# A head's 48 rows as 32 and 16: other transposes and other transfers for the attention tensors

## The chip, the cores and the metric

The kernel runs on one core of a Trainium2 chip. The metric is the device time in microseconds. Three runs of the kernel before took 797.55, 798.67 and 798.87 us (median 798.67). The profile comes from a further execution, which took 796.42 us; its span from the first to the last instruction is 794.7 us.

## The reference: what is computed

Three stages follow one another, all in fp32.

```
q, k, v, alpha: [4, 8, 768, 48]
state = alpha[t][:, None] * state + k[t][:, None] * v[t]   # 48 x 48 per head, t = 0..767
y[t]  = q[t] @ state
x = y as [3072, 384]
h = x @ w_in (384 x 2048);  g = (a0 + a1 h + a2 h^2 + a3 h^3) / (1 + |b0||h| + |b1| h^2 + 1e-6);  x = g @ w_out
h = x @ w_in2 (384 x 1024); s = h * softmax(h); x = layernorm(s) * g_ln @ w_out2
```

## The kernel before: tiles, stages and what sets the order

The sequence is cut into six chunks of 128 tokens, and each chunk into two halves of two batches; the twelve halves are numbered 0 to 11. A half has four slots of four heads, so its alpha, k and q arrive as tiles `ra`, `rk` and `rq` of 128 partitions (four slots of 32, each with four tokens in a row) by 16 x 48 values. Within a half the recurrence becomes matmuls: the running product P of alpha and its reverse scan R scale q and k (on partitions: the 48 rows of a head; along them: tokens), TensorE forms the scores `sc`, multiplies them with v into `y`, and makes the update `u` of the state `Sbd`.

For halves 0 and 1 TensorE does the transposes. For halves 2 to 11 the function `a_dve` does them on VectorE, block by block of 32 x 32 (`transpose_in`, the transposes of lines 290 and 295): they write columns four values apart, since a raw row holds four tokens. Then come the scans (lines 308 and 317), the product of k and R (line 320) and the transposes of that product back to tokens as rows (line 324), which read four values apart and write consecutively. The product of q and P is on GpSimd (line 335). Both results go through DRAM to change partitions. `kb_d` (line 329) carries the keys back into `kns` (`a_move`, line 282). `qk_d` (line 337) carries q and k into `qks` (`a_move_qk`, line 276), where the two heads of a pair lie on partitions 0 to 47 and 64 to 111 for the scores. `qk` before has three blocks per pair of heads: 32 rows of the one, 16 and 16 rows of both, 32 rows of the other.

The first network (`m_up`, `m_down`) runs 96 units of 512 tokens by 128 hidden columns: nine matmuls into `hp` (line 590), a chain on ScalarE and VectorE (lines 595 to 621), a split into `gh` on ScalarE and `gl` on GpSimd (lines 623, 624), and nine matmuls into `x2p` (line 636). Beside the early units `w1_group` loads the fp64 weights into staging tiles `st`, of which there are two by then (line 531), VectorE converts them to fp32 (lines 535 to 539), and ScalarE and GpSimd split them (lines 545, 546). The second network (lines 700 to 786) follows at the end, with transposes of its own (line 750).

The instructions of each engine run in the order in which a scheduler put them before the launch. It works from its own estimate of times, so an edit in one place can move others. SyncE (SP) issues nearly all transfers, in order: one that has to wait holds up all behind it. The pools say which tiles share memory: `ra` and `rq` are one buffer in turn, and so are the two `st`.

Of the kernel before, what the change touches and what calls it, by code (L numbers as in the profile page):

```python
# [7 lines left out]
F32 = mybir.dt.float32  # L8
# [5 lines left out]
ALU = mybir.AluOpType  # L14
# [16 lines left out]
def kernel(  # L31
# [15 lines left out]
    nc = tc.nc  # L47
# [5 lines left out]
    CH = 128  # L53
# [99 lines left out]
    def network(fast):  # L153
# [7 lines left out]
        if fast:  # L161
            att = tc.tile_pool(name="att", bufs=1, side="right")
            ap_ = att.__enter__()
            ps_a = tc.tile_pool(name="ps_a", bufs=2, space=PSUM, side="right")
            ps_ap = ps_a.__enter__()
            ident = ap_.tile([128, 128], F32, name="ident")
            nc.gpsimd.memset(ident, 0.0)
            nc.gpsimd.affine_select(
                out=ident, in_=ident, pattern=[[-1, 128]], compare_op=ALU.not_equal, fill=1.0, base=0, channel_multiplier=1
            )  # L170
            zero = ap_.tile([128, CH], BF16, name="zero")
            nc.vector.memset(zero, 0.0)
            NB6 = 6
            PER = CH + 1
            QW = 4 * CH + 2
# [28 lines left out]
        class Half:  # L204
            def __init__(self, i):
                if i == 1:
                    t = [borrow(3, 1024 * p, [B, 2 * CH]) for p in range(2)]
                    self.q = [t[p][:, :, :CH] for p in range(2)]
                    self.k = [t[p][:, :, CH:] for p in range(2)]
                    end = ap_.tile([128, B, 2], F32, name="end1")  # L210
                    self.end = [end[:, :, p] for p in range(2)]
                    self.ends = _view(end[:], 0, [[2, B], [1, 2], [0, D]])
                    self.kn = borrow(2, 0, [B * 192 + 16])
                else:
                    self.q = [qks[:, :, CH * p:CH * p + CH] for p in range(2)]
                    self.k = [qks[:, :, 256 + CH * p:256 + CH * p + CH] for p in range(2)]
                    self.end = [qks[:, :, 512 + p] for p in range(2)]
                    self.ends = _view(qks[:], 512, [[QW, B], [1, 2], [0, D]])
# [53 lines left out]

        def a_move_qk(i):
            qk, kb = moved[i]
            for m, i0, n, d0 in ((0, 0, 32, 0), (1, 0, 16, 32), (1, 16, 16, 64), (2, 0, 32, 80)):
                nc.sync.dma_start(out=qks[d0:d0 + n], in_=qk[m].rearrange("b i x -> i b x")[i0:i0 + n])
            yield

        def a_move(i):
            kb = moved.pop(i)[1]  # L280
            v_load(i)
            nc.sync.dma_start(
                out=kns[:, :B * 192].rearrange("p (b x) -> p b x", b=B), in_=kb[:].rearrange("b t x -> t b x")
            )
            yield

        def transpose_in(raw, dst, off, pstep, mstep):
            r0 = raw[:]
            for m, o in ((0, 0), (2, 192 + 16)):
                nc.vector.transpose(  # L290
                    out=_view(dst, off + m * mstep, [[pstep, 2], [1, 4], [4, 32]]),
                    in_=_view(r0, o, [[384, 2], [48, 4], [1, 32]]),
                )
            for p in range(2):
                nc.vector.transpose(
                    out=_view(dst, off + mstep + p * pstep, [[1, 4], [4, 32]]),
                    in_=_view(r0, p * 384 + 32, [[48, 4], [160, 2], [1, 16]]),
                )

        def a_dve(i):  # L300
            ra = raws.pop((i, "ra"))
            nc.vector.memset(_view(alT[:], PER, [[PER, NB6], [1, 2]]), 0.0)
            watch(i, ra)
            transpose_in(ra, alT[:], 1, 3 * PER, PER)
# [5 lines left out]
            qk = ap_.tile([128, 3, QW], F32, name="qk", tag="qk")  # L310
            qv = [_view(qk[:], x * 256, [[CH, 2], [QW, 3], [1, CH]]) for x in range(2)]
            end = _view(qk[:], 512, [[1, 2], [QW, 3]])
            nc.vector.tensor_scalar(end, _view(P[:], CH, [[3 * PER, 2], [PER, 3]]), P_MIN, None, ALU.max)
            nc.vector.reciprocal(_view(d2[:], CH - 1, [[3 * PER, 2], [PER, 3]]), end)
# [4 lines left out]
            transpose_in(raws.pop((i, "rk")), qk[:], 256, CH, QW)  # L319
            nc.vector.tensor_tensor(qv[1], qv[1], _view(R, 0, [[3 * PER, 2], [PER, 3], [1, CH]]), ALU.mult)  # L320
            yield
            kb = R[:, :768].rearrange("p (r x) -> p r x", r=4)
            for p in range(2):
                nc.vector.transpose(  # L324
                    out=_view(kb, 96 * p, [[32, 3], [192, 4], [1, 32]]),
                    in_=_view(qk[:], 256 + CH * p, [[QW, 3], [1, 4], [4, 32]]),
                )
            kb_d = dram.tile([B, CH, 192], F32, name="kb_d", tag="kb_d", bufs=2)
            nc.sync.dma_start(
                out=kb_d[:].rearrange("b (j r) x -> (b j) (r x)", r=4), in_=R[:, :768]  # L330
            )
            yield
            Pv = _view(P[:], 1, [[3 * PER, 2], [PER, 3], [1, CH]])
            transpose_in(raws.pop((i, "rq")), qk[:], 0, CH, QW)
            marks[i, 2] = nc.gpsimd.tensor_tensor(qv[0], qv[0], Pv, ALU.mult)
            qk_d = dram.tile([3, B, 32, QW], F32, name="qk_d", tag="qk_d", bufs=2)
            nc.sync.dma_start(out=qk_d[:].rearrange("m b i x -> (b i) m x"), in_=qk)
            moved[i] = (qk_d, kb_d)
            yield
        vts = {}  # L340
# [715 lines left out]
```

## Time and profile before

| | |
|---|---|
| median of three runs | 798.67 us (797.55 to 798.87) |
| profiled execution | 796.42 us, span 794.7 us |
| PE (TensorE matmul) busy | 732.0 us, 92% of the span |
| DVE (VectorE) busy | 643.2 us, 81% |
| ACT (ScalarE) busy | 535.5 us, 67% |
| POOL (GpSimd) busy | 359.5 us, 45% |
| chain that ended last | PE 45%, DVE 27%, ACT, DMA and "issue" 7% each |

The shares are means over stages of different kind. Halves 2 to 11 have their VectorE part between 44 and 460 us; from 500 us on the attention is over. A row of a timeline gives the start, the duration, the engine, the line, the operation and what it writes and reads; a duration runs to the end of an instruction, and the next one may start before that, so what an instruction takes of its engine is the distance from its start to the next one's start. In brackets stands how long the engine had been idle and what ended the wait.

### The profile page before, as it was taken

What the parts mean: (1) busy time and instruction counts of PE and PEld (TensorE: products, weight loads), DVE (VectorE), ACT (ScalarE), POOL (GpSimd) and SP (SyncE); (2) the same over time, 40 slices, a digit from 0 to 9 for tenths busy, and PEclk for the clock granted to TensorE, in tenths of its full rate; (3) what the DMA queues carried; (4) which work ended last, traced back from release to release, by engine and by line L of the source; (5) the groups of instructions that cost most, each with busy time, mean ns of one, the idle gap of its engine ahead of it and who ended that gap; (6) DMA issues with size and microseconds to landing.
All of it is one profiled execution on the core that took longest, in us unless ns stands there. A gap on an engine that the chain in (4) does not pass through costs nothing.

```text
span 794.7 us, 13903 instructions
## 1 busy us (share of the span) xinstructions
PE 732.0 (92%) x4976; PEld 606.9 (76%) x4976; DVE 643.2 (81%) x1110; ACT 535.5 (67%) x983; POOL 359.5 (45%) x306
## 2 busy tenths in 40 slices
PE   4864986999999989999999999999999999999996
PEld 3753765787777877687777788888888989998996
DVE  5999999979799998979897976567877698777630
ACT  2335756787787868788878879788775555455541
POOL 3256776856555344545454334243242524352322
PEclk9767898999999999999999999999999999999998
DMA  7956466365837275445826160460014443542552
GB/s 172 268 165 187 126 185 134 98 129 164 208 94 179 94 210 143 134 106 162 197 81 160 64 122 15 144 255 0 1 42 106 138 107 100 145 97 60 137 122 69
DMA packets 87279, 101.75 MB, mean 128 GB/s; under 512 B 34464, under 2 KB 63136, under 8 KB 87200
## 3 DMA queue, kind: packets, MB, share of 16 engines
q1 hardware_dynamic: 87104, 100.67, 48.0%
q8 instruction: 41, 0.67, 0.4%
q14 instruction: 38, 0.31, 0.1%
q10 hardware_dynamic: 96, 0.10, 0.0%
HBM read 60.59 MB, written 27.56 MB: 111 GB/s over the span
## 4 chain that ended last, share of the span: by engine, by line
PE 45%; DVE 27%; ACT 7%; DMA 7%; issue 7%; POOL 3%; SPq 3%; DVEq 0%; POOLq 0%; ACTq 0%
PE h L710 13%; PE op L774 12%; PE x2p L636 10%; PE hp L590 9%; DVE ft L539 2%; POOL gl L624 2%; SPq L266 2%; DVE p L616 2%; DVE w L619 2%; DVE alT L324 2%; DVE ft L538 2%; DVE qk L290 2%; DVE p L621 2%; DVE hp L620 2%; DVE ft L535 1%
## 5 line engine op out<-in xcount | busy, mean ns | idle before, releaser
L590 PE MATMUL hp<-xt,g 128*128 128x512 f32 x864 | 226.2, 404 | 16.7 <-DVE p L621 7.7
L590 PEld LDWEIGHTS hp<-xt,g 128*128 128x128 f32 x864 | 163.7, 193 | 59.5 <-DVE p L621 14.2
L624 POOL TENSOR_TENSOR gl<-p,gh 128x512 fp32r<-128x512 f32 x96 | 129.1, 1344 | 175.1 <-ACT gh L623 101.4
L636 PE MATMUL x2p<-gh,g 128*128 128x512 f32 x576 | 196.0, 395 | 0.6 <-ACT gh L623 0.6
L636 PEld LDWEIGHTS x2p<-gh,g 128*128 128x128 f32 x576 | 108.3, 189 | 26.3 <-ACT gh L623 1.4
L636 PE MATMUL x2p<-gl,g 128*128 128x512 f32 x288 | 113.6, 394 | 1.4 <-POOL gl L624 1.4
L774 PE MATMUL op<-w2oh,room 128*128 128x384 f32 x384 | 101.8, 339 | 0.1
L766 POOL TENSOR_TENSOR room<-room,room 128x1024 fp32r<-128x1024 f32 x22 | 53.6, 2438 | 102.2 <-ACT room L765 98.2
L619 DVE SCALAR_TENSOR_TENSOR w<-w,co,hp 128x512 f32<-128x512 f32 x84 | 61.8, 736 | 42.8 <-ACT hp L618 42.4
L710 PE MATMUL h<-w2ih,x 128*128 128x512 f32 x288 | 90.8, 394 | 0.0
L597 ACT ACTIVATE p<-hp,co 128x512 f32<-128x512 f32 x96 | 65.9, 687 | 13.9 <-POOL gl L624 13.4
L618 ACT ACTIVATE hp<-ah 128x512 f32<-128x512 f32 x84 | 50.1, 597 | 32.9 <-DVE p L616 32.2
L616 DVE SCALAR_TENSOR_TENSOR p<-p,co,hp 128x512 f32<-128x512 f32 x84 | 61.7, 734 | 12.7 <-ACT p L597 12.2
L598 ACT ACTIVATE w<-ah,co 128x512 f32<-128x512 f32 x96 | 69.3, 723 | 3.1 <-DVE hp L620 2.9
L774 PEld LDWEIGHTS op<-w2oh,room 128*128 128x128 f32 x384 | 70.0, 188 | 1.7 <-DVE room L766 0.5
L595 ACT ACTIVATE ah<-hp 128x512 f32<-128x512 f32 x96 | 56.7, 590 | 15.9 <-PE hp L590 15.8
L636 PEld LDWEIGHTS x2p<-gl,g 128*128 128x128 f32 x288 | 54.3, 189 | 14.5 <-POOL gl L624 2.6
L623 ACT ACTIVATE gh<-p 128x512 fp32r<-128x512 f32 x96 | 59.9, 624 | 8.1 <-PE x2p L636 3.0
L774 PE MATMUL op<-w2ol,room 128*128 128x384 f32 x192 | 65.0, 339 | 0.0
L621 DVE SCALAR_TENSOR_TENSOR p<-p,co,hp 128x512 f32<-128x512 f32 x84 | 62.2, 740 | 1.2
L710 PEld LDWEIGHTS h<-w2ih,x 128*128 128x128 f32 x288 | 53.9, 188 | 11.7
L617 ACT ACTIVATE ah<-w,co 128x512 f32<-128x512 f32 x84 | 60.6, 722 | 1.3
(168 smaller groups left out, 1281.1 us busy)
## 6 DMA issues: line engine op xcount, KB each, us to landing
room<-room SPq DMA_DIRECT2D x96, 128.0 KB, 2.3
qk_d<-qk SPq DMA_DIRECT2D x10, 771.0 KB, 4.0
st<-in_moe_w_in_dram SPq DMA_DIRECT2D x15, 512.0 KB, 4.9
st<-in_moe_w_out_dram SPq DMA_DIRECT2D x18, 384.0 KB, 4.2
qks<-qk_d SPq DMA_DIRECT2D x20, 257.0 KB, 5.1
x<-x_d SPq DMA_DIRECT2D x18, 256.0 KB, 3.7
out_dram<-o SPq DMA_DIRECT2D x94, 48.0 KB, 1.6
ra<-in_alpha_dram SPq DMA_DIRECT2D x44, 96.0 KB, 2.5
```

The source lines that it names most:

```text
L590: last["PE", u] = nc.tensor.matmul(hp, lhsT=w[:, kt, 128 * o:128 * o + 128], rhs=xts[c][:, kt, xx, :], start=(kt == 0 and w is hi and xx = ...
L597: nc.scalar.activation(p, hp, AF.Square, bias=co[:, 7:8])
L598: nc.scalar.activation(w, ah, AF.Square, bias=co[:, 6:7])
L616: nc.vector.scalar_tensor_tensor(p, p, a1, hp, ALU.add, ALU.mult)
L617: nc.scalar.activation(ah, w, AF.Ln, bias=rest)
L619: nc.vector.scalar_tensor_tensor(w, w, rest, hp, ALU.add, ALU.mult)
L621: fin[u] = nc.vector.scalar_tensor_tensor(p, p, a0, hp, ALU.add, ALU.mult)
L623: last["ACT", u] = nc.scalar.activation(gh, p, AF.Copy)
L624: last["POOL", u] = nc.gpsimd.tensor_tensor(gl, p, gh[:].bitcast(F32), ALU.subtract)
L636: nc.tensor.matmul(x2ps[c][d], lhsT=w[:, o, 128 * d:128 * d + 128], rhs=gg, start=(f == 0 and w is hi and gg is gh), stop=(f == NF1 - 1 an ...
L710: nc.tensor.matmul(hp[:, 512 * n:512 * n + 512], lhsT=x2s[c][:, kt, x, CH * b:CH * b + CH], rhs=w2[w][:, kt, 512 * n:512 * n + 512], start ...
L774: nc.tensor.matmul(op, lhsT=x[:, 128 * f:128 * f + 128], rhs=w2[w][:, f, :], start=(f == 0 and x is hi and w == "oh"), stop=(f == NF2 - 1 ...
```

## The change: 32 and 16 rows

Every head's 48 rows are now 32 and 16. `qk` has six blocks of 257 columns: four with 32 rows of one head each, two with 16 rows of two heads. The numbers of instructions and transfers for one of the halves 2 to 11:

| step | before | now |
|---|---|---|
| transposes of `ra`, `rk` and `rq`, each | 256, 256, 128, 128 elements | 512, 256 elements |
| transposes of the keys back | 384, 384, read four apart | 512, 128, 128, read consecutively |
| write to `qk_d` | 1 transfer | 3 transfers |
| reads from `qk_d` to `qks` | 2 of 32 rows, 2 of 16 rows | 2 of 32 rows, 4 of 16 rows |
| read from `kb_d` to `kns` | 1 transfer of 128 partitions | 4 transfers of 32 partitions |

```diff
         def a_move_qk(i):
             qk, kb = moved[i]
-            for m, i0, n, d0 in ((0, 0, 32, 0), (1, 0, 16, 32), (1, 16, 16, 64), (2, 0, 32, 80)):
-                nc.sync.dma_start(out=qks[d0:d0 + n], in_=qk[m].rearrange("b i x -> i b x")[i0:i0 + n])
+            for j in range(2):
+                nc.sync.dma_start(out=qks[64 * j:64 * j + 32], in_=qk[j].rearrange("b i x -> i b x"))
+            for j in range(2):
+                for p in range(2):
+                    nc.sync.dma_start(
+                        out=qks[64 * j + 32:64 * j + D, :, QB * p:QB * p + QB],
+                        in_=qk[2].rearrange("b i x -> i b x")[16 * p:16 * p + 16, :, QB * j:QB * j + QB],
+                    )
             yield
...
-            nc.sync.dma_start(
-                out=kns[:, :B * 192].rearrange("p (b x) -> p b x", b=B), in_=kb[:].rearrange("b t x -> t b x")
-            )
+            for g in range(4):
+                nc.sync.dma_start(
+                    out=kns[32 * g:32 * g + 32, :B * 192].rearrange("j (b x) -> j b x", b=B),
+                    in_=kb[:, :, 192 * g:192 * g + 192].rearrange("b j x -> j b x"),
+                )
+            yield
+
+        def transpose_in(raw, dst, off, step):
+            r0 = raw[:]
+            nc.vector.transpose(
+                out=_view(dst, off, [[step, 4], [1, 4], [4, 32]]), in_=_view(r0, 0, [[48, 16], [1, 32]])
             )
...
+            nc.vector.transpose(
+                out=_view(dst, off + 4 * step, [[step, 2], [1, 4], [4, 32]]),
+                in_=_view(r0, 32, [[48, 8], [384, 2], [1, 16]]),
+            )
...
             kb = R[:, :768].rearrange("p (r x) -> p r x", r=4)
-            for p in range(2):
+            nc.vector.transpose(
+                out=_view(kb, 0, [[48, 4], [192, 4], [1, 32]]), in_=_view(qk[:], CH, [[QB, 4], [1, CH]])
+            )
+            for j in range(2):
                 nc.vector.transpose(
-                    out=_view(kb, 96 * p, [[32, 3], [192, 4], [1, 32]]),
-                    in_=_view(qk[:], 256 + CH * p, [[QW, 3], [1, 4], [4, 32]]),
+                    out=_view(kb, 48 * j + 32, [[192, 4], [96, 2], [1, 16]]),
+                    in_=_view(qk[:], QB * (4 + j) + CH, [[1, CH]]),
                 )
...
             qk_d = dram.tile([3, B, 32, QW], F32, name="qk_d", tag="qk_d", bufs=2)
-            nc.sync.dma_start(out=qk_d[:].rearrange("m b i x -> (b i) m x"), in_=qk)
+            for j in range(2):
+                nc.sync.dma_start(
+                    out=qk_d[j].rearrange("b i (p x) -> (b i) p x", p=2), in_=_view(qk[:], QB * j, [[QW, 2], [1, QB]])
+                )
+            nc.sync.dma_start(out=qk_d[2].rearrange("b i x -> (b i) x"), in_=_view(qk[:], 2 * QW, [[1, QW]]))
             moved[i] = (qk_d, kb_d)
```

The edit also moves instructions, since the scheduler orders everything again. SP's queue at half 2 read like this before (`kb_d` and `qk_d` are the writes of half 2, `kns` and `qks` its reads, `ra`, `rk` and `rq` loads for half 3, `st` the loads of weight tiles):

```order
L531 DMA st<-in_moe_w_in_dram 128x512 x2
L329 DMA kb_d<-alT 128x768
L266 DMA ra<-in_alpha_dram 32x4x192 x3
L282 DMA kns<-kb_d 128x4x192
L337 DMA qk_d<-qk 128x3x514
L266 DMA ra<-in_alpha_dram 32x4x192
L531 DMA st<-in_moe_w_in_dram 128x512
L276 DMA qks<-qk_d 32x4x514
L276 DMA qks<-qk_d 16x4x514 x2
L276 DMA qks<-qk_d 32x4x514
```

The same place of SP's queue in the changed kernel:

```order
L542 DMA st<-in_moe_w_in_dram 128x512
L338 DMA kb_d<-alT 128x768
L290 DMA kns<-kb_d 32x4x192 x4
L267 DMA ra<-in_alpha_dram 32x4x192
L345 DMA qk_d<-qk 256x1x257 x2
L348 DMA qk_d<-qk 128x514
L267 DMA ra<-in_alpha_dram 32x4x192
L277 DMA qks<-qk_d 32x4x514
L267 DMA ra<-in_alpha_dram 32x4x192
L277 DMA qks<-qk_d 32x4x514
L280 DMA qks<-qk_d 16x4x257 x4
L542 DMA st<-in_moe_w_in_dram 128x512 x2
```

Of the three loads of weight tiles (`st`) that stood around this place, two came ahead of `kb_d` and one ahead of `qks`; now one comes ahead of `kb_d`, and the two others behind the last read of `qks` (one more load of `ra` stands between).

VectorE's order at half 2 before, from the transposes of the keys back on (`rq` is the last raw tile of half 2, lines 535, 538 and 539 convert weight tiles, lines 608 to 621 belong to the units):

```order
L324 STREAM_TRANSPOSE alT<-qk 128x3x4x32 x2
L295 STREAM_TRANSPOSE qk<-rq 128x4x32 x2
L539 SCALAR_TENSOR_TENSOR ft<-lent_175,fp 128x384
L290 STREAM_TRANSPOSE qk<-rq 128x2x4x32
L535 TENSOR_SCALAR ft<-st 128x512
L538 SCALAR_TENSOR_TENSOR ft<-st,ft 128x512
L539 SCALAR_TENSOR_TENSOR ft<-st,ft 128x512
L608 SCALAR_TENSOR_TENSOR hp<-p,co,hp 128x512
L535 TENSOR_SCALAR ft<-st 128x512
L616 SCALAR_TENSOR_TENSOR p<-p,co,hp 128x512
```

The same place of VectorE's order in the changed kernel, from the last transpose of `rq`:

```order
L301 STREAM_TRANSPOSE qk<-rq 128x2x4x32
L549 SCALAR_TENSOR_TENSOR fp<-lent_175,fp 128x384
L550 SCALAR_TENSOR_TENSOR ft<-st,fp 128x384
L550 SCALAR_TENSOR_TENSOR ft<-lent_175,fp 128x384
L546 TENSOR_SCALAR ft<-st 128x512
L549 SCALAR_TENSOR_TENSOR ft<-st,ft 128x512
L550 SCALAR_TENSOR_TENSOR ft<-st,ft 128x512
L619 SCALAR_TENSOR_TENSOR hp<-p,co,hp 128x512
L627 SCALAR_TENSOR_TENSOR p<-p,co,hp 128x512
L507 TENSOR_TENSOR Sbd<-u,end 48x8x48 x2
L624 SCALAR_TENSOR_TENSOR hp<-hp,co,ah 128x512
L630 SCALAR_TENSOR_TENSOR w<-w,co,hp 128x512
```

Three instructions on weight tiles that stood ahead of the last transpose of `rq` now stand behind it. The second tile `st` (`ft<-st 128x512`), which was converted between lines 608 and 616 of the first units, is now converted behind line 630, which was line 619.

## Rows read from the trace of the kernel before

**Rows 1.** Busy time by stretch: length, then each engine, clock, DMA share, GB/s.
```profile
46.00:80.00 34.00, 19.04 (x149) 14.84 (x148) 33.67 (x55) 15.86 (x32) 20.40 (x15) 0.70 0.64 173
80.00:160.00 80.00, 69.84 (x521) 53.45 (x520) 76.99 (x119) 53.69 (x100) 59.50 (x50) 0.92 0.52 138
160.00:500.00 340.00, 325.13 (x2546) 260.50 (x2546) 296.06 (x467) 275.13 (x494) 161.81 (x148) 0.99 0.51 131
500.00:754.00 254.00, 254.00 (x1220) 219.24 (x1219) 190.10 (x351) 164.94 (x308) 93.69 (x57) 1.00 0.37 104
```
**Rows 2.** Timeline of PE: start, duration, operation, idle time before and releaser.
```profile
79.67 2.04 PE L420 MATMUL sc<-qks 48*128 48x128 f32 x8 [10.56 <-DMA qks<-qk_d]
```
**Rows 3.** Who PE waited for from 160 to 500 us: total, times, longest.
```profile
PE u L483 <- DVE xt L471: 6.4, 5, 1.9
PE hp L590 <- DVE p L621: 6.0, 7, 2.2
```
**Rows 4.** Timeline of DVE at half 2: transposes and their neighbours.
```profile
46.87 1.11 DVE L290 STREAM_TRANSPOSE qk<-rk 128x256 f32<-128x256 f32 x2
47.84 0.61 DVE L295 STREAM_TRANSPOSE qk<-rk 128x128 f32<-128x128 f32 x2
48.31 0.38 DVE L295 STREAM_TRANSPOSE alT<-ra 128x128 f32<-128x128 f32 x1
...
62.66 0.55 DVE L538 SCALAR_TENSOR_TENSOR fp<-lent,fp 128x384 int32<-128x384 int32 x1
63.12 1.62 DVE L324 STREAM_TRANSPOSE alT<-qk 128x384 f32<-128x384 f32 x2
64.67 0.60 DVE L295 STREAM_TRANSPOSE qk<-rq 128x128 f32<-128x128 f32 x2
```
**Rows 5.** Timeline of DVE in the second network: its transposes.
```profile
634.82 2.36 DVE L750 STREAM_TRANSPOSE room<-room 128x1024 f32<-128x1024 f32 x2
637.10 1.24 DVE L733 SCALAR_TENSOR_TENSOR room<-room,sm,h 128x1024 f32<-128x1024 f32 x1
```
**Rows 6.** Groups by line and form: count, busy time, mean ns of one, idle before.
```profile
L290 DVE STREAM_TRANSPOSE qk<-rk 128x256 f32<-128x256 f32 x20 | 11.1, 631 | 0.0
...
L295 DVE STREAM_TRANSPOSE qk<-rk 128x128 f32<-128x128 f32 x20 | 6.3, 387 | 0.0
```
**Rows 7.** Timeline of SP at half 2: issues of transfers.
```profile
52.99 10.12 SPq L531 DMA_DIRECT2D st<-in_moe_w_in_dram  x2
...
68.12 0.45 SPq L337 DMA_DIRECT2D qk_d<-qk  x1
...
74.52 1.74 SPq L276 DMA_DIRECT2D qks<-qk_d  x4
```
**Rows 8.** Transfers by issue: count, KB each, median us from issue to landing.
```profile
st<-in_moe_w_in_dram SPq DMA_DIRECT2D x15, 512.0 KB, 4.9
...
qks<-qk_d SPq DMA_DIRECT2D x20, 257.0 KB, 5.1
...
qks<-qk_d SPq DMA_DIRECT2D x20, 128.5 KB, 4.8
```
**Rows 9.** Timeline of DVE behind half 2: weight tiles and units.
```profile
70.61 0.41 DVE L535 TENSOR_SCALAR ft<-st 128x512 int32<-128x512 int32 x1
70.94 0.73 DVE L616 SCALAR_TENSOR_TENSOR p<-p,co,hp 128x512 f32<-128x512 f32 x1
...
73.28 1.11 DVE L496 TENSOR_TENSOR Sbd<-u,end 48x384 f32<-48x384 f32 x2
...
75.15 0.76 DVE L613 SCALAR_TENSOR_TENSOR hp<-hp,co,ah 128x512 f32<-128x512 f32 x1
...
77.33 0.73 DVE L619 SCALAR_TENSOR_TENSOR w<-w,co,hp 128x512 f32<-128x512 f32 x1
```
**Rows 10.** Timeline of DVE in two later places: waits for weight tiles.
```profile
118.66 0.86 DVE L535 TENSOR_SCALAR ft<-st 128x512 int32<-128x512 int32 x1 [1.34 <-DMA st<-in_moe_w_in_dram]
...
127.75 0.40 DVE L535 TENSOR_SCALAR ft<-st 128x384 int32<-128x384 int32 x1 [1.31 <-DMA st<-in_moe_w_out_dram]
```

More of the change, by code (lines that the diff above doesn't have):

```diff
@@ L174, in network @@
             PER = CH + 1
-            QW = 4 * CH + 2
+            QB = 2 * CH + 1
+            QW = 2 * QB
             d1 = ap_.tile([128, NB6 * PER + 1], BF16, name="d1")
@@ L214, in __init__ @@
                 else:
[L215 to L218, printed above, removed]
+                    self.q = [qks[:, :, QB * p:QB * p + CH] for p in range(2)]
+                    self.k = [qks[:, :, QB * p + CH:QB * p + 2 * CH] for p in range(2)]
+                    self.end = [qks[:, :, QB * p + 2 * CH] for p in range(2)]
+                    self.ends = _view(qks[:], 2 * CH, [[QW, B], [QB, 2], [0, D]])
                     self.kn = kns
@@ L281, in a_move @@
             v_load(i)
-            nc.sync.dma_start(
-                out=kns[:, :B * 192].rearrange("p (b x) -> p b x", b=B), in_=kb[:].rearrange("b t x -> t b x")
-            )
[L285 to L292, printed above, removed]
-                )
-            for p in range(2):
[L295 to L298, printed above, removed]
+            for g in range(4):
[8 more added lines that the diff above has]
+                out=_view(dst, off, [[step, 4], [1, 4], [4, 32]]), in_=_view(r0, 0, [[48, 16], [1, 32]])
+            )
+            nc.vector.transpose(
+                out=_view(dst, off + 4 * step, [[step, 2], [1, 4], [4, 32]]),
+                in_=_view(r0, 32, [[48, 8], [384, 2], [1, 16]]),
+            )
         def a_dve(i):
@@ L303, in a_dve @@
             watch(i, ra)
-            transpose_in(ra, alT[:], 1, 3 * PER, PER)
+            transpose_in(ra, alT[:], 1, PER)
             _run(a_load(i, ("rq",)))
@@ L309, in a_dve @@
             yield
[L310 to L314, printed above, removed]
+            qk = ap_.tile([128, NB6, QB], F32, name="qk", tag="qk")
+            qv = [qk[:, :, x * CH:x * CH + CH] for x in range(2)]
+            end = _view(qk[:], 2 * CH, [[QW, 3], [QB, 2]])
+            nc.vector.tensor_scalar(end, _view(P[:], CH, [[2 * PER, 3], [PER, 2]]), P_MIN, None, ALU.max)
+            nc.vector.reciprocal(_view(d2[:], CH - 1, [[2 * PER, 3], [PER, 2]]), end)
             watch_end(i, end)
@@ L318, in a_dve @@
             yield
-            transpose_in(raws.pop((i, "rk")), qk[:], 256, CH, QW)
-            nc.vector.tensor_tensor(qv[1], qv[1], _view(R, 0, [[3 * PER, 2], [PER, 3], [1, CH]]), ALU.mult)
+            transpose_in(raws.pop((i, "rk")), qk[:], CH, QB)
+            nc.vector.tensor_tensor(qv[1], qv[1], _view(R, 0, [[PER, NB6], [1, CH]]), ALU.mult)
             yield
             kb = R[:, :768].rearrange("p (r x) -> p r x", r=4)
-            for p in range(2):
+            nc.vector.transpose(
+                out=_view(kb, 0, [[48, 4], [192, 4], [1, 32]]), in_=_view(qk[:], CH, [[QB, 4], [1, CH]])
+            )
+            for j in range(2):
                 nc.vector.transpose(
-                    out=_view(kb, 96 * p, [[32, 3], [192, 4], [1, 32]]),
-                    in_=_view(qk[:], 256 + CH * p, [[QW, 3], [1, 4], [4, 32]]),
-                )
[L328 to L331, printed above, removed]
+                    out=_view(kb, 48 * j + 32, [[192, 4], [96, 2], [1, 16]]),
+                    in_=_view(qk[:], QB * (4 + j) + CH, [[1, CH]]),
+                )
+            kb_d = dram.tile([B, 32, 768], F32, name="kb_d", tag="kb_d", bufs=2)
+            nc.sync.dma_start(out=kb_d[:].rearrange("b j x -> (b j) x"), in_=R[:, :768])
             yield
-            Pv = _view(P[:], 1, [[3 * PER, 2], [PER, 3], [1, CH]])
-            transpose_in(raws.pop((i, "rq")), qk[:], 0, CH, QW)
+            Pv = _view(P[:], 1, [[PER, NB6], [1, CH]])
+            transpose_in(raws.pop((i, "rq")), qk[:], 0, QB)
             marks[i, 2] = nc.gpsimd.tensor_tensor(qv[0], qv[0], Pv, ALU.mult)
             qk_d = dram.tile([3, B, 32, QW], F32, name="qk_d", tag="qk_d", bufs=2)
-            nc.sync.dma_start(out=qk_d[:].rearrange("m b i x -> (b i) m x"), in_=qk)
+            for j in range(2):
[3 more added lines that the diff above has]
+            nc.sync.dma_start(out=qk_d[2].rearrange("b i x -> (b i) x"), in_=_view(qk[:], 2 * QW, [[1, QW]]))
             moved[i] = (qk_d, kb_d)
```

## The prediction

> **What bounds the kernel now.** I read the busy times by stretch first, since one share for the whole span mixes stages. From 500 us on TensorE is busy in all 254 of 254 us [rows 1]; the attention is over there, so nothing in this change reaches that stage. From 80 to 160 us VectorE is busy 76.99 of 80 us, from 46 to 80 us 33.67 of 34: VectorE is the bound in both, while TensorE stands still for 10.2 and 15.0 us. From 160 to 500 us TensorE is the bound (325.13 of 340 us) and VectorE has room on the mean (296.06).
>
> Next the waits. The longest of TensorE is 10.56 us, ended by the landing of `qks` for half 2 [rows 2]. It looks like the place where an earlier `qks` pays, but VectorE is full in that stretch, and the units that TensorE would start next need it too. From 160 us on TensorE waits for two things, both on VectorE: 6.4 us in 5 waits ahead of `u`, until VectorE has emptied `y`, and 6.0 us in 7 waits ahead of `hp`, until a unit's buffer is free [rows 3]. So VectorE's time is worth all of itself up to 160 us and a part of itself, at the waits, after it.
>
> **The keys' transposes.** Before, two of 384 elements each run from 63.12 to the next start at 64.67, 1.55 us for 768 elements, 2.0 ns each [rows 4]. They read four apart and write consecutively. The second network's transposes read and write consecutively: two of 1024 run from 634.82 to 637.10, 1.11 ns per element [rows 5]. Reading the keys consecutively should bring them to that rate: 768 x 1.11 = 0.86 us, a gain of 0.69 us per half. That is the upper end, too, as no row shows a faster transpose. The lower end is a gain of 0.09 us, if it is not the distance of four that costs but something in the shape, and the 1.9 ns of the raw tiles' transposes (below) holds. I take 0.69, because the only rows with 1.1 ns are the only ones consecutive on both sides. Ten halves have it: 6.9 us of VectorE in all.
>
> The Trainium skill, page "SBUF — State Buffer", section "Door 1: The DMA port swizzle", speaks of SBUF lines of 16 bytes, of which every crossing costs unless a line is hit twice. Four fp32 are 16 bytes, so by that rule the old reads hit each line once and the new ones four times. The two rates of this trace, 2.0 against 1.11 ns, agree with it; that the line is the cause no run here shows yet.
>
> **The raw tiles' transposes.** They still write four apart, so their rate stays; the question is whether two instructions instead of four save something fixed. By durations they would: 631 ns for 256 elements and 387 ns for 128 make 1.9 ns per element and 143 ns per instruction [rows 6], six instructions fewer, 0.86 us per half. But the starts say otherwise: two of 256 take 47.84 - 46.87 = 0.97 us and two of 128 take 48.31 - 47.84 = 0.47 us [rows 4]. This is 1.9 ns per element in both with nothing fixed; the 143 ns lie beside the next instruction. I take 0 and keep 0 to 0.86 us.
>
> **The transfers.** Each half issues seven more, seventy in all: two more writes to `qk_d`, two more reads of `qks`, three more of `kns`. An issue takes 1.74 / 4 = 0.43 us of SP [rows 7]. After half 2 I cost them at nothing, since TensorE's waits there name no transfer [rows 3]; the cover is the units that run between the landing of `qks` and the scores. Without it, it is four issues on the path of `qks`, 1.7 us per half. At half 2 they are on the path. There VectorE's order puts three weight instructions behind the last `rq` transpose (63.12 - 62.66 = 0.46 us each, [rows 4]), and the keys are 0.69 us shorter, so `qk_d` can go 2.1 us before its 68.12 [rows 7]; two more writes and two more reads take 1.7 us of it back, and fewer loads of `ra` stand ahead. `qks` comes 0.4 to 3 us earlier. This is worth nothing by itself while VectorE is full.
>
> The Trainium skill, page "DMA: Bandwidth & Descriptors", section "Rules for kernel authors", speaks against these cuts: a transfer cut by partitions gains nothing, since all parts share the same engines, and one of 128 partitions is to be used. This trace agrees in that 257 KB of `qks` land after 5.1 us and 128.5 KB after 4.8 [rows 8]; half the size is not half the time. By that rule the chain at half 2 would be later, not earlier, and the sum the same, as this wait is hidden behind VectorE.
>
> **The order at half 2.** This is the cost that the diff does not show. Before, the second of three weight tiles was loaded ahead of `kb_d`: the pair of issues at 52.99 ends at 63.11 [rows 7], and VectorE converts the tile at 70.61 [rows 9]. Now its load stands behind the last read of `qks`, the third's right behind it. Those reads ended at 74.52 + 1.74 = 76.26 before; with the chain 0.4 to 3 us earlier the load goes out at 73 to 76 us and lands 4.9 us later [rows 8], at 78 to 81. VectorE, in its new order, meets this tile behind line 619 of the second unit (now 630). It reached the start of that line at 77.33; of the 6.72 us since 70.61 only 0.73 + 1.11 + 0.76 us are units and state [rows 9], so 4.1 us of weight work now stand behind it. 77.33 + 0.66 - 4.1 - 0.69 is 73.2, or 74 if the units' inputs are not earlier. So VectorE stands still from 74 to 78: 4.0 us, from 2 (all early) to 7 (tile at 81). Line 620 of that unit, the next units and the transposes of half 3 are queued behind it, and TensorE waits for those. Something comes back: two later waits for weight tiles, 1.34 and 1.31 us [rows 10], shrink for a VectorE that comes later; I take half of them, 1.3 us.
>
> **The sum.** Up to 160 us: halves 2, 3 and 4 give 3 x 0.69 = 2.1 us, the tile costs 4.0, 1.3 come back: +0.6 us. From 160 to 500 us the keys' transposes of seven halves (5 to 11) lie there; at most each takes 0.69 us from the 12.4 us of waits [rows 3], 4.8 us. I take half, 2.4 us, since some of these waits come before the keys and some end on a unit whose ScalarE part is late. After 500 us nothing. Together -1.8 us. The profiled execution took 796.42 us, 794.7 of them its span; it would be 794.6. The median of the three runs is 2.25 us above that execution, so the forecast is 798.67 - 1.8 = 796.9 us.
>
> **Rivals.**
> *The whole gain arrives.* If the second tile costs nothing, because the units behind half 2 wait for TensorE anyway, and VectorE's time counts in every half, then 6.9 us go: 791.8 us. For it: VectorE is full to 160 us, and every wait of rows 3 names it. Against it: the wait on the tile is fixed in SP's order.
> *Nothing moves.* VectorE ends its burst earlier and waits for ScalarE or TensorE instead, and the tile's wait lies in the shadow of `qks`: 798.7 us. For it: TensorE is busy for 95.6% from 160 to 500 us. Against it: the same rows up to 160 us.
> *Slower, by the late weight tile.* The tile lands at 81, VectorE stands still for 7 us and nothing comes back, because the next group's tiles are late in the same way, behind the reads of half 3: 7 - 2.1 = +4.9 us; with the 2.4 us after 160 us this makes +2.5, 801.2 us. It decides from a stop of about 5 us on. For it: all reads of `qks` wait for writes that are now three, and SP stands still with them. Against it: fewer loads of `ra` go ahead.
> *The change doesn't do what it says.* The keys keep 1.9 ns per element: then only the tile is left, 4.0 - 1.3 - 0.3 = +2.4 us, 801.1 us, beside the rival before.
>
> **How the numbers follow.** Within 0.2% (1.6 us, 797.1 to 800.3) is what a measurement of this kernel can't tell from no change. The forecast has a chance of 0.41, with a range of its own from 795 to 798.5 us, of which 0.29 lies below 797.1; the whole gain 0.16; no movement 0.20, of which 0.04 lies below; slower by the tile 0.17, by the keys' rate 0.06, together 0.23, of which 0.03 lies within the bound. Faster: 0.29 + 0.16 + 0.04 = 0.49. Slower: 0.20. Within: 0.31. I move 0.03 from faster and 0.01 from within to slower, for the order that changed in every other half and that I have not followed: 0.46, 0.30, 0.24. The range from 792.0 to 801.5 us reaches from the whole gain to both slower cases and leaves out 0.2.
>
> **What would show it.** The keys' transposes at 0.86 us per half from start to next start; the raw tiles' at 1.46 us as before; VectorE idle ahead of a weight tile between 70 and 80 us, put down to a transfer `st`; `qks` of half 2 before 79.6 us; waits of TensorE after 160 us below 12.4 us. It is wrong if VectorE shows no such idle time, if the keys take 1.5 us, or if TensorE's waits after 160 us don't shrink while VectorE is less busy there.

## The result: 0.9% slower

The changed kernel took 806.53 us (median of 6 runs, 802.65 to 807.21), the kernel before 798.77 us beside it: 1.0088 times as long, 95% interval [1.0066, 1.011] (the two medians alone give 1.0097). The forecast was 796.9 us with a range from 792.0 to 801.5: wrong by its sign, and outside its range. The profiled execution took 806.34 us, 804.5 us of it its span, 9.8 us more than the span of before.

### The profile after

Busy time by stretch, columns as in [rows 1]:

```profile
46.00:80.00 34.00, 25.71 (x177) 20.76 (x178) 28.07 (x45) 16.78 (x33) 16.37 (x16) 0.65 0.62 173
80.00:160.00 80.00, 61.78 (x488) 48.29 (x486) 75.01 (x105) 50.74 (x94) 56.49 (x47) 0.86 0.49 127
160.00:500.00 340.00, 324.31 (x2447) 260.45 (x2448) 294.24 (x438) 274.12 (x495) 161.86 (x152) 0.99 0.53 136
500.00:754.00 254.00, 254.00 (x1316) 219.29 (x1315) 191.78 (x341) 164.76 (x307) 92.75 (x58) 1.00 0.36 101
```

From 46 to 160 us VectorE, the bound of that stretch, is busy 7.6 us less than in [rows 1] (28.07 + 75.01 against 33.67 + 76.99): it stands still that much longer, and only some 1.6 us of it are saved work, the keys' transposes of three halves. After 160 us the rows are close to those of before. What it stands still for, from 40 to 165 us (total, times, longest); before, these were 1.3 + 1.3 us for weight tiles [rows 10], 0.7 us for ScalarE and 0.2 us without a known cause:

```profile
DVE ft L546 <- DMA st<-in_moe_w_in_dram: 6.9, 3, 4.1
DVE ft L546 <- POOL g L557: 1.3, 1, 1.3
DVE hp L624 <- ACT ah L621: 1.0, 1, 1.0
DVE p L627 <- ACT p L608: 0.9, 1, 0.9
```

TensorE's granted clock is lower there too (0.65 and 0.86, against 0.70 and 0.92), but none of VectorE's waits ends on TensorE; whether the clock makes ScalarE's part later is not shown.

One wait lies ahead of all this, for a weight tile near 20 us. After and before:

```profile
19.74 0.69 DVE L546 TENSOR_SCALAR fp<-lent 128x512 int32<-128x512 int32 x1 [2.03 <-DMA lent<-in_moe_w_in_dram]
```

```profile
17.74 0.70 DVE L535 TENSOR_SCALAR fp<-lent 128x512 int32<-128x512 int32 x1 [0.37 <-DMA lent<-in_moe_w_in_dram]
```

It does not follow the change: of the runs below, e7, with the work and the order of the kernel before, has 1.67 us there, and e5, with those of the changed kernel, 0.37.

The transposes of half 2 on VectorE, which answer to [rows 4]:

```profile
62.18 0.70 DVE L329 STREAM_TRANSPOSE alT<-qk 128x512 f32<-128x512 f32 x1
62.80 0.46 DVE L333 STREAM_TRANSPOSE alT<-qk 128x128 f32<-128x128 f32 x2
63.19 0.53 DVE L546 TENSOR_SCALAR fp<-lent 128x384 int32<-128x384 int32 x1
...
64.55 1.09 DVE L298 STREAM_TRANSPOSE qk<-rq 128x512 f32<-128x512 f32 x1
65.50 0.61 DVE L301 STREAM_TRANSPOSE qk<-rq 128x256 f32<-128x256 f32 x1
65.98 0.60 DVE L549 SCALAR_TENSOR_TENSOR fp<-lent,fp 128x384 int32<-128x384 int32 x1
```

From start to next start the keys take 63.19 - 62.18 = 1.01 us, against 1.55; a raw tile takes 65.98 - 64.55 = 1.43 us, against 0.97 + 0.47.

SP's issues at half 2 ([rows 7]), and what VectorE meets at the end of them ([rows 9]):

```profile
54.58 0.37 SPq L542 DMA_DIRECT2D st<-in_moe_w_in_dram  x1
63.29 0.35 SPq L338 DMA_DIRECT2D kb_d<-alT  x1
65.64 2.35 SPq L290 DMA_DIRECT2D kns<-kb_d  x4
...
68.56 1.30 SPq L345 DMA_DIRECT2D qk_d<-qk  x2
...
74.71 1.71 SPq L280 DMA_DIRECT2D qks<-qk_d  x4
76.46 0.42 SPq L267 DMA_DIRECT2D ra<-in_alpha_dram  x1
76.98 0.85 SPq L542 DMA_DIRECT2D st<-in_moe_w_in_dram  x2
```

```profile
77.10 0.75 DVE L630 SCALAR_TENSOR_TENSOR w<-w,co,hp 128x512 f32<-128x512 f32 x1
81.91 0.43 DVE L546 TENSOR_SCALAR ft<-st 128x512 int32<-128x512 int32 x1 [4.07 <-DMA st<-in_moe_w_in_dram]
...
120.36 0.53 DVE L546 TENSOR_SCALAR ft<-st 128x512 int32<-128x512 int32 x1 [2.00 <-DMA st<-in_moe_w_in_dram]
...
130.83 0.62 DVE L546 TENSOR_SCALAR ft<-st 128x512 int32<-128x512 int32 x1 [0.83 <-DMA st<-in_moe_w_in_dram]
```

The second and third tile go out together behind the last reads of `qks`, and VectorE waits 4.07 us in front of line 546, behind line 630. The scores start at 77.80 us against 79.67 [rows 2]: the first reads of `qks` are earlier by 1.9 us, and VectorE, the bound, gains nothing by it. The issue of the last reads, which the tiles stand behind, ends at 74.71 + 1.71 = 76.42 us, against 76.26 before.

Where the loss is made: by unit 78 (515 us) the changed kernel is 5.2 us behind, and so it is at the first output tile. Ahead of that the lag of single units can't be read as a loss, since the new order places units and attention differently: by the ends of ScalarE's `gh` it is 6.4 us at unit 15, 15.4 at unit 18 and 4.4 at unit 40. The first and the last output tile, ScalarE's timeline, show the rest. Before:

```profile
625.63 0.47 ACT L783 ACTIVATE o<-op 128x384 f32<-128x384 f32 x1
...
787.67 0.49 ACT L783 ACTIVATE o<-op 128x384 f32<-128x384 f32 x1 [3.75 <-PE op L774]
```

After:

```profile
630.87 0.48 ACT L794 ACTIVATE o<-op 128x384 f32<-128x384 f32 x1
...
797.14 0.49 ACT L794 ACTIVATE o<-op 128x384 f32<-128x384 f32 x1 [3.74 <-PE op L785]
```

5.2 us late at the first, 9.5 us at the last: 4.2 us are lost in the second network, which the change does not touch and where the order of VectorE's and TensorE's instructions is the same in both kernels. There, VectorE's short operations of 0.15 us behind a tile's norm read, before:

```profile
649.94 2.14 DVE L745 TENSOR_TENSOR sm<-sm 128x1 f32<-128x1 f32 x1 [0.79 <-ACT sm L744]
652.11 0.16 DVE L746 SCALAR_TENSOR_TENSOR sm<-sm 128x1 f32<-128x1 f32 x1
652.30 0.16 DVE L747 SCALAR_TENSOR_TENSOR sm<-sm 128x1 f32<-128x1 f32 x1
652.50 0.82 DVE L748 TENSOR_SCALAR room<-room,sm 128x1024 f32<-128x1024 f32 x1
```

After, with GpSimd's subtractions beside them in the second fence:

```profile
656.08 2.15 DVE L756 TENSOR_TENSOR sm<-sm 128x1 f32<-128x1 f32 x1 [1.62 <-ACT sm L755]
658.26 2.33 DVE L757 SCALAR_TENSOR_TENSOR sm<-sm 128x1 f32<-128x1 f32 x1
660.62 0.16 DVE L758 SCALAR_TENSOR_TENSOR sm<-sm 128x1 f32<-128x1 f32 x1
660.81 2.78 DVE L759 TENSOR_SCALAR room<-room,sm 128x1024 f32<-128x1024 f32 x1
```

```profile
655.80 7.25 POOL L777 TENSOR_TENSOR room<-room,room 128x1024 fp32r<-128x1024 f32 x3 [18.57 <-ACT room L776]
```

Three of these four operations (lines 756, 757 and 759) stand for some 2 us longer than their like; the first two end with a subtraction of GpSimd, the third 0.55 us behind one. Before, one did. The trace of e5 (below) has the same three held, and between its first and its last output the same 166.3 us, against 162.0 before.

### The profile page after: what moved, and what is told of

Its sections match the earlier page's. It is cut to its first block, busy times and chain, and to the rows that moved or that the text cites. A ratio compares the mean times of both kernels' runs of the same rounds, so it can differ in the third digit from the quotient of the medians.

```text
span 804.5 us, 13967 instructions
## 1 busy us (share of the span) xinstructions
PE 735.0 (91%) x4976; PEld 612.7 (76%) x4976; DVE 639.5 (79%) x1060; ACT 534.3 (66%) x983; POOL 352.9 (44%) x306
## 4 chain that ended last, share of the span: by engine, by line
DVE 43%; PE 19%; ACT 12%; DMA 11%; issue 7%; SPq 4%; POOL 3%; DVEq 0%; ACTq 0%; POOLq 0%
PE hp L601 7%; PE x2p L647 6%; DMA st<-in_moe_w_in_dram 4%; DVE room L761 3%; DVE w L630 3%; DVE room L744 3%; DVE ft L550 2%; DVE p L627 2%; DVE P L314 2%; PE op L785 2%; ACT jk L746 2%; DVE hp L631 2%; DVE room L759 2%; DVE sm L740 2%; DVE alT L323 2%
## 5 line engine op out<-in xcount | busy, mean ns | idle before, releaser
L601 PE MATMUL hp<-xt,g 128*128 128x512 f32 x864 | 229.3, 408 | 26.2 <-DVE p L632 16.2
L601 PEld LDWEIGHTS hp<-xt,g 128*128 128x128 f32 x864 | 166.6, 196 | 68.0 <-DVE p L632 19.5
L606 ACT ACTIVATE ah<-hp 128x512 f32<-128x512 f32 x96 | 56.7, 591 | 11.8 <-PE hp L601 11.2
```

Source lines behind the costliest of these rows:

```text
L601: last["PE", u] = nc.tensor.matmul(hp, lhsT=w[:, kt, 128 * o:128 * o + 128], rhs=xts[c][:, kt, xx, :], start=(kt == 0 and w is hi and xx = ...
```

## The experiments

Since the change moves both the work and the order that the scheduler makes of it, most experiments hold one of them. All instructions of the program are chained in a given order on each engine, by edges that order the issue and wait for nothing (code in this part is shortened):

```
     network(True)
+    in_order(tc)
+def in_order(tc):
+    by = {i.name: i for i in tc.nc.cur_bb.bb.instructions}
+    for names in ORDER:   # one list of instruction names per engine
+        for a, b in zip(names, names[1:]):
+            tc.add_manual_dep(by[b], a, DependencyInfo(NoSync, DATA), reason="order")
```

Times are medians; the ratio is that to the kernel before beside it (798.2 to 798.6 us), with its 95% interval, and can differ a little from the ratio of the medians.

### Work and order apart (e1, e2)

e1 is the changed kernel with ORDER taken from the kernel before, e2 the kernel before with ORDER taken from the changed one.

> The changed kernel's instructions, with each engine's order fixed to that of the kernel before (the merged transposes at the place of the last of the four). If the order is what costs (the theory): the 0.54 us per half that the keys' transposes now save count, and nothing stands late; 794 to 798 us, no wait of VectorE for a weight tile between 70 and 85 us above 1 us. If the seventy more and smaller transfers cost (rival): they are all still there, 803 to 808 us, with waits on qks or kns. If the second network's tail loses its 4.3 us by chance of when it starts (second rival): 799 to 803 us with the last operations of the tail late as in the changed kernel.

> The kernel before's instructions (six transposes per raw pair of tensors, strided reads of the keys, the fewer transfers), with each engine's order fixed to that of the changed kernel. Theory (order): as slow as the changed kernel or slower by the 0.54 us per half that is given up, 805 to 811 us, VectorE waiting about 4 us for the second weight tile near 78 us. Rival (transfers): 797 to 801 us.

e1: 803.01 us, 1.0043 [1.0021, 1.0065]; nine runs lie from 802.3 to 805.3, three from 797.0 to 799.0, which stays unexplained. e2: 808.76 us, 1.0141 [1.0114, 1.0167]. So neither theory has it alone. The new order costs the old work ten microseconds, and the new work is slower in the old order as well; the two costs do not add up, as both together are 7.8 us. In e1 VectorE waits for weight tiles more than in any other kernel (total, times, longest, 40 to 165 us):

```profile
DVE ft L546 <- DMA st<-in_moe_w_in_dram: 6.8, 3, 4.6
DVE ft L546 <- DMA st<-in_moe_w_out_dram: 4.1, 2, 3.6
```

Between e2 and the changed kernel, which share the order, only the work differs: e2 is 0.4 us ahead near 168 us and 5.8 us behind near 470 us. These 6.2 us are more than the keys' transposes save in seven halves, 7 x 0.54 = 3.8 us; what the rest is stays open.

### SP's order alone (e3)

The changed kernel with ORDER for all engines, SP's from the kernel before, the others' its own.

> The changed kernel with only the DMA queue's order on SP that of the kernel before, all other engines in the changed kernel's order. If the late weight tiles behind the reads of qks are the cause within the order: VectorE's wait of 4.07 us at 78 us goes, and 4 to 8 us come back, 798 to 802 us. If it is the order on VectorE and TensorE (rival): 804 to 808 us, though that wait is gone.

803.44 us, 1.0073 [1.0053, 1.0093]: between the two, and its trace says why. VectorE still waits 5.7 us for weight tiles, and the first output comes only 0.7 us earlier than in the changed kernel. The last is 4.0 us earlier: the other 3.3 us come from the second network, where two short operations of VectorE stand and not three. For the first network, SP's order alone as the cause within the order fell.

### The transfers alone (e4)

```
-for m, i0, n, d0 in ((0, 0, 32, 0), (1, 0, 16, 32), (1, 16, 16, 64), (2, 0, 32, 80)):
+for m, i0, n, d0 in ((0, 0, 16, 0), (0, 16, 16, 16), (1, 0, 16, 32), (1, 16, 16, 64), (2, 0, 16, 80), (2, 16, 16, 96)):
-    dma_start(out=kns, in_=kb)                 # one read
+    for g in range(4): dma_start(out=kns[32 * g:32 * g + 32], in_=kb[:, 32 * g:32 * g + 32])
-    dma_start(out=qk_d, in_=qk)                # one write
+    for m in range(3): dma_start(out=qk_d[m], in_=qk[:, m])
```

> The kernel before, its order fixed, with its transfers cut into as many as the changed kernel has (qk_d in 3, qks in 6, kns in 4) and nothing else. Theory (order): the transfers are covered from half 3 on, and cost 1.7 us or less at half 2, of which VectorE hides most: 798 to 800.5 us. Rival (transfers): 803 us or more, TensorE's waits on qks grown by 1.7 us and more per half.

These cuts are as many as the change's, not the same ones: `qks` is cut by rows only, and `kns` by tokens. 803.77 us, 1.0075 [1.0054, 1.0095]: 5.1 us for seventy transfers, the theory (covered, at most 2 us) fell. Its SP and VectorE at half 2 show the way it goes:

```profile
69.11 1.77 SPq L282 DMA_DIRECT2D kns<-kb_d  x4
70.93 1.40 SPq L337 DMA_DIRECT2D qk_d<-qk  x3
72.38 0.58 SPq L266 DMA_DIRECT2D ra<-in_alpha_dram  x1
73.05 0.63 SPq L531 DMA_DIRECT2D st<-in_moe_w_in_dram  x1
```

```profile
79.84 0.43 DVE L535 TENSOR_SCALAR ft<-st 128x512 int32<-128x512 int32 x1 [2.51 <-DMA st<-in_moe_w_in_dram]
```

Before, `kns` and `qk_d` took one issue each from 67.63 to 68.57 us and the tile's load went out at 70.06; here they take seven, it goes out at 73.05, and VectorE waits 2.51 us for it. Summed over 40 to 165 us it waits for weight tiles 8.3 us against 2.7. TensorE's wait for `qks` of half 2 is longer as well, 12.7 us against 10.6. The first output comes at 631.13 us, 5.5 us later than before: the loss is in the first network.

### The weight tiles' loads elsewhere (e5 to e8, e11)

The 14 loads of groups 2 and 3 move from SP to ScalarE, each right behind ScalarE's copy of the tile that leaves the buffer (all other instructions by ORDER): in the changed kernel's own order (e5), with the new work in the old order (e6), in the kernel before (e7), and with the keys' part of the change alone in the old order (e8). e11 is e8 with GpSimd in place of ScalarE.

```
-nc.sync.dma_start(out=st[:, :n], in_=src)
+(nc.scalar if fast and keep is None and not stage["wide"] else nc.sync).dma_start(out=st[:, :n], in_=src)
```

> The changed kernel, its own order on every engine, with one thing moved: the 14 loads of weight tiles of groups 2 and 3 are issued by ScalarE (each right behind ScalarE's copy of the tile that leaves the buffer) and no longer by SP behind the attention's transfers. Theory (weight tiles late because they queue on SP): VectorE's 4.07 us at 78 us and the waits of 2.0 and 0.8 us near 120 and 131 us go, and more comes back than by SP's old order alone (803.4 us): 797 to 802 us. Rival (VectorE's and TensorE's new order): 803 to 806 us although these waits are gone.

> The changed kernel's instructions in the order of the kernel before, with the same 14 loads on ScalarE's queue. Theory: the seventy more transfers cost only by the loads queued behind them; with these elsewhere the keys' transposes give a gain: 793 to 798 us against 803.0 with the loads on SP. Rival (the transfers cost by their own landing, on qks and kns): 800 us or more, TensorE's wait on qks of half 2 above 12 us.

> The control: the kernel before, its own order, with the same 14 loads on ScalarE's queue. Theory: only its own two waits (1.34 and 1.31 us) can go: 796 to 799 us. If the move itself is what gains in the other two (rival), it gains here as much: 793 us or less. If issuing on ScalarE costs: 800 us or more.

> Of the change only the keys: two transposes of 384 with consecutive reads, kb_d by rows, kns in 4 reads; raw tiles, qk_d and qks as in the kernel before, its order, and the 14 loads on ScalarE's queue. Theory: the keys' transposes fall from 1.55 to about 0.9 us per half, three transfers more per half cost nothing: 793 to 797 us, the best of the four. Rival (VectorE's gain does not count): as e7, 796 to 799 us.

> Of the change only the keys, as in e8, in the order of the kernel before, with the 14 loads issued by GpSimd (each ahead of its subtraction of the tile that leaves the buffer) instead of ScalarE. Theory: ScalarE is no longer held by the loads (in e8 VectorE waited 1.76 us for it), and the weight tiles are on time: 794 to 797 us, below the kernel before. Rival (issuing on GpSimd costs more than it gives): 798 us or more.

| | us | ratio to before |
|---|---|---|
| e5 changed, own order | 801.94 | 1.0053 [1.0033, 1.0074] |
| e6 new work, old order | 801.67 | 1.0048 [1.0032, 1.0065] |
| e7 kernel before | 798.88 | 1.0014 [1.0004, 1.0024] |
| e8 keys alone, old order | 797.23 | 1.0001 [0.9986, 1.0016] |
| e11 as e8, on GpSimd | 806.43 | 1.0107 [1.0079, 1.0136] |

e5 came within its range, but in its profiled execution, one of its two slowest (805.65 us), the first output is 0.7 us later than the changed kernel's: the first network shows no gain there. e6 missed, and its trace shows the sign of the rival. VectorE waits 5.0 us for a tile at 126 us and 5.9 us for ScalarE at 87 us; ScalarE had waited for TensorE's scores, and TensorE 14.57 us for `qks` of half 2, against 10.56 [rows 2]:

```profile
83.54 3.06 PE L431 MATMUL sc<-qks 48*128 48x128 f32 x16 [14.57 <-DMA qks<-qk_d]
85.63 0.60 ACT L438 ACTIVATE A<-sc 128x512 f32<-128x512 f32 x1 [6.52 <-PE sc L431]
87.17 1.17 DVE L298 STREAM_TRANSPOSE qk<-rk 128x512 f32<-128x512 f32 x1 [5.86 <-ACT jk L237]
```

So in the old order the new work's transfers cost by their own issues and landing too, and not only by what is queued behind them. e11 missed more: GpSimd stands 8.9 us at the loads until VectorE has emptied their tiles, and VectorE waits 7.3 us for weight tiles. e8 missed its range by 0.2 us and can't be told from the kernel before. What stands is the difference between these kernels: the keys' part, three transfers included, is worth 1.65 us by the medians (e8 against e7), though the intervals of the two ratios overlap, and with the rest of the change 4.4 us are lost (e6 against e8), whose intervals lie apart. That cost lies with the raw tiles, `qk_d` and `qks`; these runs do not part the three.

### No loads to be late (e9, e10, e13)

Groups 2 and 3 are converted from one small tile; 13 loads fall away (the weights are not the reference's), in the old order.

```
-st = moe_pool.tile([128, NTOK], I64, name="st", tag="st", bufs=2)
-nc.sync.dma_start(out=st[:, :n], in_=src)
-w32 = st[:, :n].bitcast(I32).rearrange("p (n t) -> p n t", t=2)
+if x == 14: nc.sync.dma_start(out=stx, in_=moe_w_in[0:128, 0:16])
+w32 = _view(stx[:].bitcast(I32), 0, [[0, n // 16], [2, 16], [1, 2]])
```

> The changed kernel's instructions in the order of the kernel before; 13 of the 14 loads of weight tiles of groups 2 and 3 are left out, and all 14 tiles are converted from one small tile (128 x 16) instead, so that VectorE has the same instructions and never waits for a weight tile (the weights are then not those of the reference). Theory (the seventy more transfers cost only by the weight tiles behind them): 1.5 to 3 us faster than e10, the keys' gain, so 792 to 796 us. Rival (they cost by the landing of qks, or by the transfers' own traffic): not faster than e10 or slower.

> The control for e9: the kernel before, its order, with the same 13 loads left out in the same way. Both theories: its two waits of 1.3 us go, 795 to 798 us.

> The kernel before, its order, its transfers cut into as many as the changed kernel's (as in e4), and the 13 loads of weight tiles left out (as in e9 and e10, the weights are then not those of the reference). Theory (the transfers cost only by the weight tiles queued behind them): 792.5 to 794 us, as e10 (792.93). Rival (they have a cost of their own, on qks and on what shares the DMA engines): 795 us or more, TensorE's waits on qks longer than in e10 by as much.

e10, old work: 792.93 us. e9, new work: 793.99, within its range, but 1.1 us slower than e10 and not faster. e13, old work with the more transfers: 796.52, from 792.4 to 799.0 in 12 runs. All three missed. The loads cost the kernel before itself 5.3 us, more than its two waits; and the transfers keep 3.6 of their 5.1 us by the medians (e13 against e10). The traces part these 3.6 us. In the trace of e13 (796.44 us) VectorE waits for no transfer from 40 to 165 us, and its units from 180 to 270 us end 0.2 to 0.3 us behind e10's. The first and the last output of e10 (the first two rows) and of e13:

```profile
623.73 0.47 ACT L783 ACTIVATE o<-op 128x384 f32<-128x384 f32 x1
...
784.50 0.49 ACT L783 ACTIVATE o<-op 128x384 f32<-128x384 f32 x1 [3.67 <-PE op L774]
624.51 0.47 ACT L783 ACTIVATE o<-op 128x384 f32<-128x384 f32 x1
...
788.10 0.49 ACT L783 ACTIVATE o<-op 128x384 f32<-128x384 f32 x1 [3.67 <-PE op L774]
```

With the loads gone the transfers cost 0.8 us in the first network, where with them they cost 5.5 (e4 against the kernel before); the other 2.8 us of e13 are lost in the second, where two of the short operations behind a tile's norm stand beside GpSimd's subtractions, and in e10 one. So in e4 the loss in the first network goes with the weight loads, by this one pair of traces. Of the 4.4 us of e1, 3.3 go with the loads by the medians (1.1 are left between e9 and e10); the first output of e9 comes at 623.68 us, level with e10's.

### The held operations (e12, e14)

```
-    FASTS = (0, 20)
+    FASTS = (0, 4, 5, 6, 20)
```

> The changed kernel with the low-half subtractions of tiles 4, 5 and 6 of the second network on VectorE instead of GpSimd (one constant; before 640 us nothing moves). Theory (three of VectorE's short operations at 656 to 661 us stand 2.2 us each while GpSimd subtracts, and this sets back the end): the 4.3 us that the last output loses after 640 us shrink to about 1, 801 to 804 us against 806.5. Rival (the reads of room land late): 805 us or more, the short operations at 0.16 us but the end as late.

> The kernel before with the subtractions of tiles 4, 5 and 6 on VectorE, as in e12. In the kernel before one short operation of VectorE stands there for 2.1 us and not three. Theory: 0 to 2 us faster, 796.5 to 798.5 us. Rival (the move gains by itself whatever stands held): 795 us or less, as much as the 3.3 us of e12.

e12 (changed kernel): 803.23 us, 1.0062 [1.0045, 1.0079], 3.3 us less than the changed kernel by the medians; the two intervals still touch, and it is the trace that places the gain. e14 (before): 798.41 us, 0.9992 [0.9979, 1.0005], no gain. Both as the theory had it. The operations of e12 beside the two fences above, and its last output, 4.05 us earlier though the first is only 0.32 us earlier:

```profile
655.25 1.23 DVE L777 TENSOR_TENSOR room<-room,room 128x1024 fp32r<-128x1024 f32 x1 [1.22 <-ACT room L776]
656.39 0.15 DVE L756 TENSOR_TENSOR sm<-sm 128x1 f32<-128x1 f32 x1
...
656.74 0.15 DVE L757 SCALAR_TENSOR_TENSOR sm<-sm 128x1 f32<-128x1 f32 x1
```

```profile
630.55 0.47 ACT L794 ACTIVATE o<-op 128x384 f32<-128x384 f32 x1
...
793.09 0.49 ACT L794 ACTIVATE o<-op 128x384 f32<-128x384 f32 x1 [3.75 <-PE op L785]
```

### What the change is good for (e15, e16)

The keys alone, in the old order:

```
-in_=_view(qk[:], 256 + CH * p, [[QW, 3], [1, 4], [4, 32]]),
+in_=_view(qk[:], 256 + CH * p, [[QW, 3], [1, CH]]),
-kb_d = dram.tile([B, CH, 192], F32, ...)
+kb_d = dram.tile([B, 32, 768], F32, ...)
-dma_start(out=kns, in_=kb.rearrange("b t x -> t b x"))
+for g in range(4): dma_start(out=kns[32 * g:32 * g + 32], in_=kb[:, :, 192 * g:192 * g + 192].rearrange("b j x -> j b x"))
```

> Of the change the keys alone in the order of the kernel before, the weight tiles' loads on SP as they were. Theory: three more transfers ahead of the third weight tile make it 1.3 us later, the keys' transposes give 0.6 us per half: 797 to 799 us, VectorE waiting 1 to 2 us for the tile near 78 us. Rival (three transfers already cost what seven cost): 802 us or more.

> Of the change the keys alone in the order of the kernel before, the 14 loads on ScalarE (e8), and the three subtractions on VectorE (e12, e14). Theory: e8's 797.2 less what its two held operations cost at the end, about 1 us: 795 to 797 us, below both kernels. Rival (the end is set by TensorE and not by these): as e8, 797 us or more.

e16: 798.85 us, 1.0001 [0.9985, 1.0016], no change; in its trace VectorE waits 0.7 us for weight tiles, less than forecast. e15, with the loads on ScalarE and the three subtractions on VectorE: 796.45 us, 0.9969 [0.9955, 0.9983]. It is the one version with the reference's weights that lies clearly below both kernels.

## Why the prediction was wrong, by its steps

*The keys' transposes, 0.69 us per half.* Right in kind, the size 0.54. The one of 512 runs at 1.21 ns per element (0.62 us to the next start), near the 1.11 of [rows 5]; the two of 128, in runs of 16, take 0.39 us, 1.5 ns.

*The raw tiles, nothing.* Right: 1.43 us against 1.44.

*`qks` of half 2 earlier by 0.4 to 3 us, hidden.* Right for the scores, 1.9 us, hidden. Wrong for the end of the reads, where the weight tile queues: 76.42 against 76.26 us.

*The late weight tile, 4.0 us.* Right in kind, and 4.07 us by luck. The prediction had VectorE standing from 74 to 78 us, and it stood from 77.8 to 81.9. The load went out at 76.98 us, not at 73; and VectorE was through with line 630 at 77.8 and not at 74, as it had waited 3.6 us for GpSimd and ScalarE since 67 us. Two errors of nearly 4 us cancel.

*"Something comes back: two later waits for weight tiles shrink", 1.3 us.* Wrong, and this is the first failed term of the sum. The later waits are 2.00 and 0.83 us, 2.8 together against 2.65. The group that follows queues behind the next half's transfers as this one did. The rival "slower, by the late weight tile" said so; it was priced at +2.5 us.

*The transfers after half 2, nothing.* Wrong. The prediction looked for them in TensorE's waits [rows 3] and took their absence as cover. Cut alone they cost 5.1 us (e4). Most of it goes by the weight tiles that queue behind them on SP, and shows in VectorE's waits: without these loads 0.8 us of 5.5 are left in the first network (e13). They also cost by their own landing, in e6, where the scores of half 2 wait 14.57 us for `qks`.

*Up to 160 us, +0.6.* This sum failed. VectorE's idle time from 46 to 160 us is 7.6 us longer, of which 4.2 are weight tiles and the rest mostly GpSimd and ScalarE (1.3, 1.0, 0.9 us), which the new order puts in its way; against that stand three halves of 0.54 us, which leaves 6.0 us. Another 1.7 us are the longer wait near 20 us, which does not follow the change. Of the 5.2 us that are left at the first output, how much is this wait stays open: e13, with 2.46 us there, is within 0.3 us of e10, with 0.27, from 180 us on. Of the new order the prediction followed one instruction, the tile's load, and gave the rest 0.04 of chance; held fixed, that order costs the old work more than anything else here (e2, +10.1 us). Which of its instructions do it in the first network is not shown: SP's order alone (e3) and the loads alone (e5) give back next to nothing there.

*160 to 500 us, -2.4.* Right in size where the order is the same: with the keys alone in the old order the lag falls from 3.0 to 0.5 us (e8). In the changed kernel itself it can't be read, as units and attention lie differently. The sign it was to be known by failed: TensorE's idle time there is 15.7 us, against 14.9 before [rows 1]. In the new order, the same seven halves give 6.2 us against e2, more than the transposes account for.

*After 500 us, nothing.* Wrong by 4.2 us. TensorE is busy all 254 us there in both kernels, and yet the end is later: three of VectorE's operations stand beside three of GpSimd's subtractions, before it was one. e12 took that away and gave back 3.3 us of the median, 3.7 of the 4.2 us in its trace. That they meet because the stage starts 5.2 us later is argued, not shown; e2 starts it 11.2 us later and has two held.

*The rule of the Trainium skill* from the page "DMA: Bandwidth & Descriptors", section "Rules for kernel authors", that speaks against cutting transfers, which the prediction weighed and hid behind VectorE, was the one to follow. The cut cost 5.1 us (e4), most of it by the queue of issues; that the parts share the same engines, the page's reason, is not what these runs show. That of the page "SBUF — State Buffer", section "Door 1: The DMA port swizzle", agrees with 2.0 against 1.2 ns per element; the 1.5 ns of the two short transposes it does not give, and that the line of 16 bytes is the cause no run here shows.

## What to carry to other kernels

An extra transfer costs by what is queued behind it on its queue and by its own landing, so look for its price in the waits of every engine that this queue serves, and follow each wait back to its start: a wait of VectorE for ScalarE was a wait for a transfer in e6. When a change lets a scheduler order the program anew, measure the order by itself: the same work in the old order, and the old work in the new. A stage that the change doesn't touch can still lose time, if it holds short operations that can fall on another engine's long ones. And a number that comes out right can be two errors that cancel: compare the start and the end of a wait with the forecast, not only its length.

## What had not been expected of the hardware

- VectorE's operations of 0.15 us on a 128x1 tile stood 2.14 to 2.33 us, and one of 0.81 us stood 2.78, while GpSimd subtracted 128x1024 tiles (2.4 us each). In the same stretch VectorE's transposes (1.25 us), its reductions (1.20 us) and its operations with an operand in PSUM (1.28 us) ran at their usual time. Nor were all short operations held: lines 731 and 732 took 0.14 and 0.16 us at 657.06 and 657.24 us of the kernel before, beside a subtraction from 655.79 to 658.20. What parts the two kinds no run here tests. With the subtractions off GpSimd the held ones took 0.15 us (e12).
- VectorE's wait for the weight tile near 20 us differs between traces, and not by the change: 0.37 us before, 2.03 in the changed kernel, 2.02 in e1, 0.29 in e2, 1.67 in e7, 2.07 in e16 and 2.46 in e13. Runs of one kernel spread over up to 8.3 us (e1), more than the 0.2% that the prediction took as the limit of what can be told.
- Moving 14 loads of 512 or 384 KB to GpSimd's queue cost 9.2 us against ScalarE's (e11, e8).
